# Load depth, store times, the first chunk turned by DMA, and planned landings in a fused recurrence and MoE kernel

## The chip, the cores and the metric

One Trainium2 chip; the kernel runs on one of its cores. The metric is the device time of one execution in microseconds (us). TensorE is called PE, VectorE DVE, ScalarE ACT, GpSimd POOL and SyncE SP, as the profile does.

## The reference

First a gated linear recurrence over 4 batches, 8 heads, 768 steps and heads of 48; then, on its output as 3072 tokens of 384, two dense layers (384 to 2048 to 384) with a squared ReLU between them.

```python
# recurrence: state is (B, H, D, D)
for t in range(S):
    state = alpha[:, :, t, :, None] * state + np.einsum('bhd,bhe->bhde', k[:, :, t], v[:, :, t])
    y[:, :, t] = np.einsum('bhd,bhde->bhe', q[:, :, t], state)
# x: y as (3072, 384)
h = x @ w_in            # 384 x 2048
r = np.maximum(h, 0.0)
out = (r * r) @ w_out   # 2048 x 384
```

## The kernel before, in words

**Chunks.** The 3072 tokens are 24 chunks of 128 (`NT`), six per batch. Chunks 0 to 3 are done as two "supers" (`add_super`), the others one at a time (`add_chunk`), from chunk 8 on with the scores of two chunks together. For a chunk, four operands of 128 x 384 floats are loaded by SP (`add_load`, L369: at, qt, kt, vt, 192 KB each). ACT takes the logarithm of at (L439), PE sums it along the chunk with a triangular matrix, and ACT makes the exponential of that and of its negative (`A` or `Af` L467, `Ainv` L471). DVE multiplies q and k by them into `qk_s` (L495 or L498, and L501). `qk_s` is turned (transposed) into `qkT`; PE makes the scores `sc` from it, DVE masks them into `sm` (L570), and PE sums masked scores times v, and q times the state, into the chunk's output. The state is carried by `st`: PE adds k times v, DVE multiplies it by the chunk's whole decay `ae_s` (`stm`, L604), ACT casts it (L609).

**The decay.** For chunks before `TURN` = 12, `ae_s` is made by small matmuls and exponentials. From 12 on it is copied out of the last row of `Af` by two small DMAs that POOL issues (`e_aed`, L484). `Af` has two buffers, so a chunk's `Af` waits until these DMAs of the chunk two before have read theirs.

**The turns.** A chunk's output is cast to `xn` (ACT, L395) and turned into its columns of `xT_big`, from which the first dense layer reads. Chunks 4 to 13 have both turns, `qk_s` to `qkT` and `xn` to `xT_big`, done by PE with an identity (8 and 3 transposes, L276) and a copy out of PSUM by DVE (L397). From `XFROM` = 14 on both are DMA transposes that SP issues (L515 and L416), in the same queue as the loads.

**The dense layers.** They run in groups of chunks (4, 1, 1, then pairs: `GN`). `add_moe1` is the first layer (PE), its ReLU (ACT, L876) and square into `gT` (DVE, L884); `add_moe2` the second (PE), the copy out of PSUM into `held` (L949 or L951) and the store (L959 or L962), which POOL issues except for the last three chunks. Their PE work lies between that of the chunks.

**What sets the order.** Nothing is reordered at run time: the order of every engine's instructions is written out by a planner (`Plan`) when the kernel is built. Each operation has an engine, a duration, a latency after it (`lat`), what it depends on, and perhaps an earliest time (`at`). The planner takes the operation that can start first; a wrong latency makes an engine stand in front of an instruction whose input has not come, with everything behind it in its order. The places that matter here:

- Loads: `LB` chunks can be loaded at once (pairs of chunks in `LB // 2` buffers for each of the four operands). In the plan a load waits for the chunk `LB` before (`prev`), and from chunk 14 on also for the one `LB - 1` (seven) before (`pace`).
- `AE_LAT`: what the plan assumes from the end of POOL's issue of `ae_s` to its landing. `XLAT` is the same for `qkT` (and, less 0.8, for `xT_big`); SP's issue of a turn counts as 1.25, and a turn is planned 2.0 after its inputs (`XB_SLACK`).
- `OUT_AT`: the earliest time of POOL's store of chunk s is `OUT_AT + 2.5 * s`. Until it is stored, an output stays in `held`, four buffers of four chunks each, of one kind with the buffers that the weights pass through.
- The gate: chunk s's first matmul may be planned when s is at most a lead plus the MoE work planned so far, in chunks (one chunk is 5.12 us of PE in the plan). The lead is 3.5, and more for later chunks, up to 6.

```python
return s <= (LEAD if s < 10 else min(6.0, LEAD + 0.25 * (s - 9))) + (prog["m1"] + prog["m2"]) / 5.12
```

A chunk also shares its slot of `qk_s` and `ae_s` with the chunk four before (`NBUF` = 4) and begins only when that one has its `xn`.

Of the kernel before, what the change touches and what calls it, by code (L numbers as in the profile page):

```python
# [59 lines left out]
def after(op, x=0.0):  # L60
    return (op, x)
# [103 lines left out]
def kernel(  # L165
# [21 lines left out]
    NT = n_tok // P  # L187
# [10 lines left out]

    consts = ctx.enter_context(tc.tile_pool(name="consts", bufs=1))
    big = ctx.enter_context(tc.tile_pool(name="big", bufs=1))  # L200
    LB = 8
    XR = 10
    loads = ctx.enter_context(tc.tile_pool(name="loads", bufs=LB // 2))
    work = ctx.enter_context(tc.tile_pool(name="work", bufs=4))
# [48 lines left out]

    NBUF = 4
    TURN = 12
    AE_LAT = 2.0
    L_s = big.tile([P, NBUF, H, DP], BF16)
    nc.gpsimd.memset(L_s[:, :, :, D:], 0.0)
    qk_s = big.tile([P, NBUF, 2, H, DP], BF16)
# [9 lines left out]
    def pin(ins):  # L269
        tc.keep_in_program_order(ins)  # L270

    def mm(*a, **kw):
        pin(nc.tensor.matmul(*a, **kw))  # L273

    def tr(*a):
        pin(nc.tensor.transpose(*a))  # L276
# [11 lines left out]
    def psum(op, shape, dt):  # L288
        i = op.slot.bank
        return banks[i].tile(shape, dt, name=f"bank{i}")  # L290
    X_SLACK = 0.2
    LD = 1.05
# [4 lines left out]
    def add(eng, dur, emit, *deps, **kw):  # L297
        return plan.add(Op(eng, dur, emit, deps, **kw))
# [42 lines left out]
    def w_dep(which, f):  # L341
        return w_ready[which][[hi > f for hi in W_CUT[which][1:]].index(True)]

    C = [dict() for _ in range(NT)]
# [1 line left out]
    SRC = dict(srcs)  # L346
    EARLY = 2 * 3
    PAIRS = 8
    XFROM, XTO = 14, NT
    XLAT = 2.2  # L350
    LEAD = 3.5

    NS = 2
# [6 lines left out]
    def add_load(s, nm):  # L360
        d = C[s]
        b, c = divmod(s, NCH)
        k = s // 2

        def ld():
            if s % 2 == 0:
                PAIR[k][nm] = loads.tile([P, 2, H, D], FP32, name=nm)
            d[nm] = PAIR[k][nm][:, s % 2]
            pin(nc.sync.dma_start(out=d[nm], in_=SRC[nm][b, c]))  # L369
        prev = C[s - LB]["use_" + nm] if s - LB >= 2 * NS else None  # L370
        if 2 * NS <= s < 2 * NS + LB and (k - LB // 2) < NS:
            prev = SUP[k - LB // 2]["use_" + nm]
        pace = C[s - LB + 1]["use_" + nm] if s >= TURN + 2 else None
        d["ld_" + nm] = add("DMA", LD if s < 12 else 0.95, ld, prev, pace, lat=2.4)

    PAIR = [dict() for _ in range(NT // 2)]
    SRC2 = [("at", alpha), ("qt", q), ("kt", k), ("vt", v)]
# [15 lines left out]
    def cast(op, out_t, in_t):  # L393
        if op.eng == "ACT":
            pin(nc.scalar.copy(out_t, in_t))  # L395
        elif op.eng == "DVE":
            pin(nc.vector.tensor_copy(out_t, in_t))  # L397
        else:
            pin(nc.gpsimd.tensor_copy(out_t, in_t))

    def add_tail(s, done, first, g):
        d = C[s]

        def e_xn():
            d["xn"] = work.tile([P, HD], BF16, name="xn")
            cast(xn, d["xn"], d["py"][:, 0:HD])
        xn = add("ACT", 0.36, e_xn, done, **g)
        first.gives = xn

        def e_p4():  # L410
            d["px"] = psum(p4, [P, KT, P], BF16)
            for j in range(KT):
                tr(d["px"][:, j, :], d["xn"][:, j * P:(j + 1) * P], ident_bf)
        if XFROM <= s < XTO:
            def e_xturn():
                pin(nc.sync.dma_start_transpose(out=xT_big[:, :, s % XR * P:(s % XR + 1) * P], in_=d["xn"]))  # L416
            d["x"] = add("XB", 0.0, e_xturn, xn, lat=XLAT - 0.8)
            d["x"].turn = 0.4
            d["end"] = xn
            return  # L420
        p4 = plan.add(Op("PE", 0.165, e_p4, [xn], takes=GLA_BANKS, lat=0.14, **g))

        def e_xT():
            cast(xT, xT_big[:, :, s % XR * P:(s % XR + 1) * P], d["px"])
        xT = add({"ACT": 0.36, "DVE": 0.27} if s < EARLY else "DVE", 0.27, e_xT, p4, prio=-9.0)
        d["x"] = d["end"] = xT
        p4.gives = xT

    def add_chunk(s):
        d = C[s]  # L430
# [57 lines left out]
        else:  # L488
            p0.gives = ai
            ae1 = add("POOL", 1.03, e_aed, a_, lat=AE_LAT, prio=-20.0)  # L490
            ae1.dma = 0.3
# [10 lines left out]
        mq = d["use_qt"] = add("DVE", 0.47 if s < TURN else 0.78, e_qA, a_, d["ld_qt"], old, **g)  # L502
        mk = d["use_kt"] = add("DVE", 0.47, e_kI, ai, d["ld_kt"], old, **g)
# [16 lines left out]
        def e_cp(lo, hi):  # L520
            if lo == 0:
                d["qkT"] = work.tile([P, 2 * NP, P], BF16, name="qkT")
            cast(cpk if lo else cp, d["qkT"][:, lo:hi, :], d["pT"][:, lo:hi, :])
        if s < EARLY:
            cp = add({"ACT": 0.49, "DVE": 0.34}, 0, lambda: e_cp(0, NP), p1q, **g)
            cpk = add({"DVE": 0.34, "ACT": 0.49}, 0, lambda: e_cp(NP, 2 * NP), p1k, after(cp, -9.0), **g)
        elif s < XFROM:
            cp = cpk = add("DVE", 0.61, lambda: e_cp(0, 2 * NP), p1k, **g)
        else:
            cp = cpk = add("XB", 0.0, e_turn, mq, mk, lat=XLAT)  # L530
            cp.turn = 0.9
        if s < XFROM:
            p1q.gives = cpk
# [47 lines left out]
    def add_back(s):  # L581
# [47 lines left out]
        p3b = plan.add(Op("PE", 0.21, e_p3b, [after(sm1, 0.02), sm0, vb, after(p3a)], takes=None if c else GLA_BANKS, lat=0.15, **g))  # L629

        add_tail(s, p3b, p3a or p3b, g)

    def add_super(u):
# [206 lines left out]
    NGT = 3  # L840
    FIRST = sl_bank[4:1:-1]
    M2_LAST = sl_bank[::-1]
    OUT_AT = 104.0
    LAST_COLS = ((0, 256), (256, 384))
    RELU_PRIO = -20.0
    RELU_PRIO0 = 0.0
# [4 lines left out]
    prog = {"m1": 0.0, "m2": 0.0}  # L851
# [69 lines left out]
    def add_moe2(g, tt, before, box, quarters, pools):  # L921
        if GT[g] + tt == NT - 1:
            return add_last(g, tt, before, pools)

        for qd in quarters:
            def e_mm(qd=qd):
                if qd == 0:
                    box["po"] = psum(box["first"], [P, 512], FP32)[:, 0:d_model]
                for kf in range(qd * FT // NQ, (qd + 1) * FT // NQ):
                    mm(box["po"], lhsT=gT[g][:, kf, tt * P:(tt + 1) * P], rhs=w_out_b[:, kf, :],  # L930
                       start=(kf == 0), stop=(kf == FT - 1))
            fs = range(qd * FT // NQ, (qd + 1) * FT // NQ) if g == 0 else range(FT)
            deps = [o for f in fs for o in sq[(g, f)]] + [w_dep("o", fs[-1] if g == 0 else FT - 1)] + ([after(before)] if before else [])
            op = plan.add(Op("PE", 0.65, e_mm, deps, takes=pools if qd == 0 else None, prio=0.1))
            op.moe = (2, 2.56 / NQ)
            if qd == 0:
                box["first"] = op
            op.lat = 0.05
            before = op
        if quarters[-1] < NQ - 1:  # L940
            return op
        s = GT[g] + tt

        def e_ev():
            if s % 4 == 0:
                held[s // 4] = stage.tile([P, 4, d_model], FP32, name="held", tag="stage")
            box["ob"] = held[s // 4][:, s % 4]
            if ev.eng == "DVE":
                pin(nc.vector.tensor_copy(box["ob"], box["po"]))  # L949
            else:  # L950
                pin(nc.scalar.copy(box["ob"], box["po"]))  # L951
        ev = add({"DVE": 0.47, "ACT": 0.38}, 0, e_ev, op, prio=-15.0)
        box["first"].gives = ev

        q = nc.gpsimd if s < NT - 3 else nc.sync

        def e_out():
            if s >= 2 * NS:
                pin(q.dma_start(out=out_r[s], in_=box["ob"]))  # L959
            else:  # L960
                for t in range(2):
                    pin(q.dma_start(out=out2_r[s, t], in_=box["ob"][HF * t:HF * t + HF]))  # L962
        if s < NT - 3:
            add("POOL", 0.56, e_out, ev, at=OUT_AT + 2.5 * s, lat=2.5, prio=5.0).dma = 0.55
        else:
            add("OUT", 0.55, e_out, ev)
        return op

    DMA_ORDER = ["0 at0 qt0 kt0 at1 qt1 kt1 vt", "1 at0 at1 qt0 kt0 qt1 kt1", "i", "1 vt"] + ["i"] * 5 + ["o"] * 4
    for x in DMA_ORDER + [s for s in range(2 * NS, NT) if s not in DMA_ORDER]:  # L970
        if x in ("i", "o"):
            load_w(x)
        elif isinstance(x, str):
            for nm in x[1:].split():
                add_load2(int(x[0]), nm)
            if len(SUP[int(x[0])]) == 2 * len(srcs) - 1:
                add_super(int(x[0]))
        else:
            for nm, _ in srcs:
                add_load(x, nm)  # L980
            add_chunk(x)
# [23 lines left out]
    def gate(op):  # L1005
        s = getattr(op, "gla", None)
        if s is not None:
            return s <= (LEAD if s < 10 else min(6.0, LEAD + 0.25 * (s - 9))) + (prog["m1"] + prog["m2"]) / 5.12
        return True

    def on_pick(op):
        m = getattr(op, "moe", None)
        if m:
            prog["m1" if m[0] == 1 else "m2"] += m[1]
    plan.on_pick = on_pick
    plan.run(gate)


# [47 lines left out]
```

## Time and profile before

| | |
|---|---|
| median of 3 runs | 182.1 us (181.08 to 182.48) |
| the profiled execution | 183.13 us |
| its span, first to last instruction | 181.4 us |
| PE / DVE / ACT / POOL busy | 96% / 69% / 68% / 29% of the span |
| granted PE clock, mean | 0.998 |
| read from HBM, written | 25.17 MB, 4.72 MB |
| transfers on SP's queue, on POOL's | 76.7%, 7.4% of 16 engines' span |

A row of the profile names engine, line of the kernel, operation, and out<-in by the program's names. "Busy" is the time in which an engine executed; matmuls are pipelined and their ends are modelled, so a row's mean is longer than the pace at which they follow each other. PEld are the weight loads that overlap the matmuls, and SPq is SP's sequencer, which issues DMAs. Idle time is put down to what ended the last wait. DMA share is the mean busy share of 16 DMA engines.

### The profile page before, as it was taken

The numbers are of one execution on the slowest core, as the hardware profiler recorded it, in microseconds if no ns is written. First come the engines' busy times: TensorE is split into PE (matmuls) and PEld (weight loads), VectorE is DVE, ScalarE is ACT, GpSimd is POOL, SyncE is SP. The second block draws the span as 40 slices with busy tenths as digits, with TensorE's granted clock in tenths as the row PEclk, the third lists the DMA queues.
The fourth block names the chain that finished last, engine by engine and source line by source line (L and its number), as shares of the span: only waits on it lengthen the run. The fifth ranks groups of instructions, "written<-read, shape, count | busy, mean of one in ns | idle before, by whom it ended". The sixth has DMA issues, their size and how long they took to land.

```text
span 181.4 us, 4845 instructions
## 1 busy us (share of the span) xinstructions
PE 173.3 (96%) x1883; PEld 127.1 (70%) x1883; DVE 124.5 (69%) x258; ACT 122.6 (68%) x263; POOL 53.5 (29%) x95
## 2 busy tenths in 40 slices
PE   7899999999999999999898999999997999999993
PEld 3567774666996788879676665787756767787663
DVE  6699569538898889989896875598754943455000
ACT  3565879267998599879586945698955843686221
POOL 6024466611121111133061257553290411010200
PEclk9999999999999999999999999999999999999999
DMA  5999999899998989999999999999998543210122
GB/s 139 274 276 325 338 290 383 201 214 207 190 200 167 226 173 216 198 227 180 201 208 142 191 214 163 266 231 158 243 170 213 117 97 107 47 47 0 43 87 90
DMA packets 113687, 33.83 MB, mean 186 GB/s; under 512 B 107728, under 2 KB 111952, under 8 KB 113664
## 3 DMA queue, kind: packets, MB, share of 16 engines
q1 hardware_dynamic: 111424, 29.37, 76.7%
q0 software_dynamic: 2240, 4.15, 7.4%
q8 instruction: 15, 0.25, 0.6%
q14 instruction: 8, 0.07, 0.1%
HBM read 25.17 MB, written 4.72 MB: 165 GB/s over the span
## 4 chain that ended last, share of the span: by engine, by line
PE 81%; DMA 8%; DVE 7%; ACT 1%; issue 1%; DVEq 0%; ACTq 0%
PE bank L273 73%; PE bank L276 5%; DMA qkT<-qk_s 3%; DMA xT_big<-xn 3%; DVE sm L570 2%; PE sc L273 2%; PE st L273 2%; DMA qt<-in_q_dram 2%; DVE sm L762 1%; DVE qkT L397 1%; DVE qk_s L699 1%; ACT r L876 1%; DVE xT_big L397 0%; DVE st L604 0%; DVE qk_s L495 0%
## 5 line engine op out<-in xcount | busy, mean ns | idle before, releaser
L273 PE MATMUL bank<-xT_big,w_in_b 128*128 128x256 bf16 (+2 forms) x600 | 71.6, 268 | 2.1 <-DMA xT_big<-xn 1.5
L273 PE MATMUL bank<-w_out_b,gT 128*128 128x384 bf16 (+2 forms) x400 | 69.8, 319 | 0.0
L876 ACT ACTIVATE r<-bank 128x512 bf16<-128x512 f32 x96 | 56.4, 612 | 11.1 <-PE bank L273 9.1
L273 PEld LDWEIGHTS <-w_in_b 128*128 128x128 bf16 x600 | 53.1, 98 | 12.5 <-issue 3.1
L884 DVE TENSOR_TENSOR gT<-r 128x512 bf16<-128x512 bf16 x96 | 43.5, 482 | 13.2 <-ACT r L876 12.8
L273 PEld LDWEIGHTS <-gT 128*128 128x128 bf16 x400 | 36.8, 98 | 19.7 <-issue 0.2
L444 POOL CAST vb<-vt 128x384 bf16<-128x384 f32 x20 | 11.5, 574 | 51.3 <-PE bank L273 25.5
L951 ACT COPY held<-bank 128x384 f32<-128x384 f32 x22 | 10.6, 483 | 17.9 <-PE bank L273 17.8
L484 POOL DMA_DIRECT2D ae_s<-Af x24 | 12.2, 513 | 22.1 <-ACT Af L467 20.3
L570 DVE TENSOR_TENSOR sm<-sc,utri_b 128x512 bf16<-128x512 f32 x24 | 15.4, 683 | 4.3 <-PE sc L273 4.2
L959 POOL DMA_DIRECT2D out_dram<-held x17 | 9.3, 549 | 26.0 <-ACT held L951 26.0
L395 ACT CAST xn<-bank 128x384 bf16<-128x384 f32 x24 | 11.2, 486 | 7.3 <-PE bank L273 7.2
L498 DVE TENSOR_TENSOR qk_s<-qt,Af 128x384 bf16<-128x384 f32 x12 | 10.3, 858 | 7.6 <-ACT Af L467 7.6
L273 PEld LDWEIGHTS <-qkT 64*128 64x128 bf16 (+2 forms) x304 | 10.6, 97 | 6.0 <-issue 2.3
L439 ACT ACTIVATE L_s<-at 128x384 bf16<-128x384 f32 x20 | 10.6, 530 | 2.4 <-DMA at<-in_alpha_dram 2.4
L604 DVE TENSOR_TENSOR st<-st,ae_s 128x384 f32<-128x384 f32 x16 | 9.0, 561 | 4.7 <-DMA ae_s<-Af 2.5
L397 DVE COPY qkT<-bank 128x1024 bf16<-128x1024 bf16 (+1 forms) x16 | 9.7, 619 | 3.3 <-PE bank L276 3.2
L467 ACT ACTIVATE Af<-bank 128x384 f32<-128x384 f32 x12 | 10.7, 893 | 1.4 <-DMA ae_s<-Af 0.8
L609 ACT CAST sb<-st 128x384 bf16<-128x384 f32 x16 | 7.9, 496 | 5.3 <-DVE st L604 5.0
L501 DVE TENSOR_TENSOR qk_s<-kt,Ainv 128x384 bf16<-128x384 f32 x20 | 11.3, 563 | 0.2 <-ACT Ainv L471 0.2
L276 PE MATMUL bank<-ident_bf,qk_s 128*128 128x128 bf16 x112 | 10.2, 224 | 0.5 <-DVE qk_s L699 0.3
L471 ACT ACTIVATE Ainv<-bank 128x384 bf16<-128x384 f32 x20 | 10.5, 525 | 0.0
(71 smaller groups left out, 168.8 us busy)
## 6 DMA issues: line engine op xcount, KB each, us to landing
at<-in_alpha_dram SPq DMA_DIRECT2D x24, 192.0 KB, 3.9
qt<-in_q_dram SPq DMA_DIRECT2D x24, 192.0 KB, 3.8
kt<-in_k_dram SPq DMA_DIRECT2D x24, 192.0 KB, 3.9
vt<-in_v_dram SPq DMA_DIRECT2D x20, 192.0 KB, 3.9
out_dram<-held POOLq DMA_DIRECT2D x17, 192.0 KB, 3.5
wo<-in_moe_w_out_dram SPq DMA_DIRECT2D x4, 768.0 KB, 7.9
wi<-in_moe_w_in_dram SPq DMA_DIRECT2D x4, 384.0 KB, 7.1
wi<-in_moe_w_in_dram SPq DMA_DIRECT2D x2, 768.0 KB, 6.1
```

Source lines behind the costliest of these rows:

```text
L273: pin(nc.tensor.matmul(*a, **kw))
L276: pin(nc.tensor.transpose(*a))
L395: pin(nc.scalar.copy(out_t, in_t))
L397: pin(nc.vector.tensor_copy(out_t, in_t))
L439: pin(nc.scalar.activation(L[:, :, 0:D], d["at"], AF.Ln))
L444: pin(nc.gpsimd.tensor_copy(d["vb"], d["vt"]))
L467: pin(nc.scalar.activation(d["A"], split(d["pm"][:, 0:HD], s), AF.Exp))
L484: pin(nc.gpsimd.dma_start(out=ae_s[HF * j:HF * j + D, i, j], in_=d["Af"][P - 1:P, j]))
L501: pin(nc.vector.tensor_mul(kI[:, :, 0:D], d["kt"], d["Ai"]))
L570: pin(nc.vector.tensor_mul(d["sm"][:, hh], d["sc"][hh], utri_b.to_broadcast([P, NP, P])))
L876: pin(nc.scalar.activation(box["r"][:, 0:w], box["ph"][:, 0:w], AF.Relu))
L884: pin(nc.vector.tensor_mul(gT[g][:, f0:f0 + per, lo * P:lo * P + n], r, r))
```

## The change

Loads are ten chunks deep instead of eight, and the plan no longer paces them by the chunk seven before; the condition for the first reused buffers counts from 0. Chunks 14 and 15 are turned by PE like those before them, both `qk_s` and `xn`; turns by DMA begin with chunk 16. In the plan, `ae_s` lands 3.6 us after its issue instead of 2.0, `qkT` 2.8 (3.6 for chunks 16 to 19) instead of 2.2, `xT_big` 2.0 instead of 1.4. Stores by POOL may go from 118 + 2.0 s on instead of 104 + 2.5 s. The lead stays at 3.5 up to chunk 11 and then grows by 0.4 a chunk instead of 0.25 from chunk 10 on: it is smaller than before for chunks 10 to 14 and larger for 15 to 18.

```diff
-    LB = 8
+    LB = 10
...
-    AE_LAT = 2.0
+    AE_LAT = 3.6
...
-    XFROM, XTO = 14, NT
-    XLAT = 2.2
+    XFROM, XTURN = 16, 16
+    XLAT = 2.8
...
         prev = C[s - LB]["use_" + nm] if s - LB >= 2 * NS else None
-        if 2 * NS <= s < 2 * NS + LB and (k - LB // 2) < NS:
+        if 0 <= k - LB // 2 < NS:
             prev = SUP[k - LB // 2]["use_" + nm]
-        pace = C[s - LB + 1]["use_" + nm] if s >= TURN + 2 else None
-        d["ld_" + nm] = add("DMA", LD if s < 12 else 0.95, ld, prev, pace, lat=2.4)
+        d["ld_" + nm] = add("DMA", LD if s < 12 else 0.95, ld, prev, lat=2.4)
...
-        if XFROM <= s < XTO:
+        if s >= XTURN:
             def e_xturn():
...
-            cp = cpk = add("XB", 0.0, e_turn, mq, mk, lat=XLAT)
+            cp = cpk = add("XB", 0.0, e_turn, mq, mk, lat=XLAT + (0.8 if s < 20 else 0.0))
             cp.turn = 0.9
...
-    OUT_AT = 104.0
+    OUT_AT = 118.0
...
-            add("POOL", 0.56, e_out, ev, at=OUT_AT + 2.5 * s, lat=2.5, prio=5.0).dma = 0.55
+            add("POOL", 0.56, e_out, ev, at=OUT_AT + 2.0 * s, lat=2.5, prio=5.0).dma = 0.55
...
-            return s <= (LEAD if s < 10 else min(6.0, LEAD + 0.25 * (s - 9))) + (prog["m1"] + prog["m2"]) / 5.12
+            return s <= (LEAD if s < 12 else min(6.0, LEAD + 0.4 * (s - 11))) + (prog["m1"] + prog["m2"]) / 5.12
```

## The prediction

> **What bounds the kernel now.** I began with the busy line of the page, then cut the span into stages, then asked who makes TensorE (PE) wait. All rows are of the profiled execution of the kernel before.
>
> ```profile
> PE 173.3 (96%) x1883; PEld 127.1 (70%) x1883; DVE 124.5 (69%) x258; ACT 122.6 (68%) x263; POOL 53.5 (29%) x95
> ```
>
> PE is the bound. The stages (start:end, length, then busy time and count for PE, weight load, DVE, ACT, POOL, then granted clock, DMA share, GB/s) show where its few idle microseconds lie:
>
> ```profile
> 60.00:94.00 34.00, 33.41 (x400) 26.77 (x399) 30.22 (x64) 27.48 (x59) 7.38 (x13) 1.00 1.03 202
> 94.00:104.00 10.00, 9.46 (x80) 7.02 (x77) 7.83 (x17) 8.49 (x18) 2.85 (x7) 1.00 1.06 174
> ...
> 118.00:128.00 10.00, 9.64 (x103) 8.26 (x102) 9.13 (x20) 9.04 (x20) 3.84 (x8) 1.00 1.09 205
> 128.00:140.00 12.00, 10.54 (x95) 7.18 (x93) 6.65 (x14) 7.84 (x17) 5.26 (x10) 1.00 1.06 211
> 140.00:150.00 10.00, 10.00 (x116) 7.17 (x115) 7.11 (x15) 6.22 (x13) 3.19 (x6) 1.00 0.45 98
> ```
>
> Up to 140 us the sixteen DMA engines are full (share above 1: records overlap); after that DMA is half idle and PE has no gap. Between 60 and 140 us PE idles 0.59 + 0.54 + 0.36 + 1.46 = 2.95 us (104 to 118 has none). That is nearly all that this change can win back. PE's own waits name the releasers (total, times, longest):
>
> ```profile
> PE bank L273 <- DMA xT_big<-xn: 1.5, 1, 1.5
> ...
> PE bank L273 <- ACT r L876: 0.7, 2, 0.5
> PE bank L273 <- DVE sm L570: 0.5, 1, 0.5
> PE bank L273 <- DMA qkT<-qk_s: 0.4, 1, 0.4
> ```
>
> Two are turns by DMA that land late, in this timeline of PE (start, length, then the idle time before in brackets):
>
> ```profile
> 124.99 0.40 PE L273 MATMUL sc<-qkT 64*128 64x128 bf16 x8
> 125.75 0.40 PE L273 MATMUL bank<-qkT 64*128 64x128 bf16 x8 [0.36 <-DMA qkT<-qk_s]
> ...
> 135.14 0.81 PE L273 MATMUL bank<-w_out_b,gT 128*128 128x384 bf16 x4
> 137.42 1.14 PE L273 MATMUL bank<-xT_big,w_in_b 128*128 128x256 bf16 x9 [1.46 <-DMA xT_big<-xn]
> ```
>
> The other two come from ae_s, the decay that chunks from 12 on move by a POOL DMA. At 87.29 DVE's `stm` (L604) waits for it, and the masks `sm` queued behind come late: 0.51 us on PE at 90.03. And the exponential `Af` (L467) has two buffers, so chunk 16's waits until chunk 14's ae has landed; in ACT's order a relu stands behind it, and PE then waits 0.54 us for that relu's bank at 99.63:
>
> ```profile
> 98.30 0.85 ACT L467 ACTIVATE Af<-bank 128x384 f32<-128x384 f32 x1 [0.80 <-DMA ae_s<-Af]
> 98.94 1.12 ACT L876 ACTIVATE r<-bank 128x512 bf16<-128x512 f32 x2
> ```
>
> **Two more turned chunks on PE (14 and 15).** Each adds 8 transposes of qk_s and 3 of xn. In the chain of waits such runs stand as
>
> ```profile
> 38.67 0.45 PE bank L276 x8
> ...
> 53.80 0.17 PE bank L276 x3
> ```
>
> so 0.45 + 0.17 = 0.62 us a chunk, **+1.24 us** for two. PE has no spare room there, so all of it counts. DVE gets two copies to qkT (0.68 us in its rows) and two to xT_big (0.35): 2.1 us, hidden, since between 94 and 104 us DVE is busy 7.83 of 10; at worst, without that cover, 2.1 us more. POOL and ACT get nothing.
>
> The Trainium skill speaks against this step: "TensorE: Matmul & The Clock Gate", Part 4 (PE-mode transpose), gives about 275 ns for one 128x128 transpose inside a kernel; by it the step would cost 6.1 us instead of 1.24. The trace has a mean of 224 ns from start to end, but eight in a row took 0.45 us, so they overlap.
>
> **Four turns fewer by DMA.** They free the SP queue of two issues of 1.64 us and two of 1.21 (medians of L515 and L416), 5.7 us. What they free on the DMA engines I read where nearly nothing else uses SP's queue, 140 to 160 us (packets, MB, share):
>
> ```profile
> q1 hardware_dynamic: 2720, 0.66, 20.3%
> ```
>
> Five turns of 0.66 MB took 20.3% of 20 us, 4.06 us. The four removed ones move 0.72 MB (two of 262 KB, two of 98 KB), so 4.4 us. The Trainium skill ("Advanced Engine Details and Errata", X-Bar Transpose) calls such turns as fast as plain DMAs and expects 350 to 400 GB/s, by which they would free about 2 us; the rows give 163 GB/s here.
>
> **Loads ten deep, without pace.** In 60 to 94 us, 35 loads took 101.8% of 34 us on q1: 0.99 us each. Loads already ran at that rate; only from 94.7 us, when SP began to interleave turns, were they spread out, the last landing at 133.9. Seventeen loads were left then: 16.8 us, plus two qk turns of 1.6 us, so they would now end near 115. They are not held up by buffers: load s needs chunk s-10's operands, and chunk 13's were multiplied at 84 us.
>
> **Stores held.** The first store was issued at 104.71, planned at 104, so planned times hold. Now stores go from 118 on at one per 2.0 us. Before, 118 to 134 us saw 8 stores, now 8 or 9: no fewer, but the loads are gone. In 140 to 160 us POOL's queue moved 0.99 MB in 15.0% of 20 us, so a store of 192 KB is 0.6 us of the engines; 118 to 140 us would carry 11 stores (6.6 us), five turns of qk_s (1.6 each) and six of xn (0.6 each): 18 of 22 us, where the share was 1.06 to 1.09.
>
> **Landings planned longer.** The medians from issue to landing were
>
> ```profile
> ae_s<-Af POOLq DMA_DIRECT2D x24, 0.8 KB, 3.6
> ...
> qkT<-qk_s SPq DMA_TRANSPOSE x10, 4.6
> xT_big<-xn SPq DMA_TRANSPOSE x10, 3.9
> ```
>
> against plans of 2.0 (after 1.03 of issue) for ae, 1.25 + 2.2 for qkT and 1.25 + 1.4 for xT_big. The new plans are 3.6, 1.25 + 2.8 (3.6 before chunk 20), and 1.25 + 2.0. So PE and DVE place the consumers later, with other work ahead: at 135 us four chunks' second-layer work (chunks 14 to 17) was there to be done. Of the three waits on qkT, xT_big and sm (0.36 + 1.46 + 0.51 = 2.33) I take 2.1 as gone. Nothing of PE's work goes, so that is the whole gain: **-2.1 us**.
>
> **Chunks begin later (10 to 13), then earlier (16 to 18).** By the gate, chunk 11 starts after 7.5 instead of 7.0 chunks' worth of MoE work, chunk 16 after 10.5 instead of 10.75. The later ones are covered by MoE work: at 90 us four chunks of second-layer work (8 to 11) were open, 10 us. Chunk 16 moves nearer to chunk 14: 1.2 chunk's worth instead of 1.5. Their `Af` stood 5.9 us apart, 0.8 of it the wait; 5.1 x 1.2 / 1.5 = 4.1 leaves a wait of 1.7. No row shows that wait at its new length: between -0.5 (ae lands sooner without turns beside it, and the wait goes) and +1.8 (the relu is as much later as ACT waits, and the chunk is early by the full quarter of MoE work, some 1.8 us with the recurrence in between). I take **+0.4**, half the added wait, since a bank of three was still free for part of the old one.
>
> **Sum:** +1.24 - 2.1 + 0.4 = -0.5 us. The profiled execution took 183.13 us, span 181.4; the median shown is 182.1, 1.0 below it. 183.1 - 0.5 is 182.6 for that execution, and **181.6** on the median.
>
> **Rivals.**
> *All waits go.* If the relu's wait goes too, and no new one appears: -2.95 + 1.24 = -1.7, and each removed wait also gives back the restart of PE (135.14 + 0.65 for four matmuls to 137.42 is 1.63, not 1.46; four times 0.16 = 0.6): -2.3, 179.8 us. For it: every wait has a DMA behind it, and that resource is relieved. Against: another order brings waits of its own. Chance 0.15.
>
> *The waits only move.* The turns of the pair (16,17) now meet the dense loads, as the pair (18,19) did, and wait as long; only sm's 0.5 goes, the ACT wait stays: +1.24 - 0.5 + 0.4 = +1.1, 183.2 us. Chance 0.16.
>
> *Slower: turns stuck behind loads.* SP issues in order, and nothing paces the loads any more. With two loads of 0.9 us ahead and the longest landing traced (6.2 for qkT, 5.6 for xT_big), a turn arrives 8.0 or 7.4 us after its input, against 6.85 and 5.25 that the plan allows (2.0 of slack, issue, landing): 1.2 + 2.1 = 3.3 us on the pair (16,17). With the gains kept: -0.5 + 3.3 = +2.8, **184.9 us**. It decides when more than one load stands ahead of a turn whose input is ready. For it: 105.32 to 111.31 for chunk 17's turn, with loads in flight. Against: it had stores beside it too, which are now gone from that stage. Chance 0.17.
>
> *Transposes that don't overlap.* At their 224 ns, 22 cost 4.9 us: 185.3 us. The row of eight in 0.45 us speaks against it. Chance 0.02. (It is the rule of the Trainium skill's "TensorE" page, Part 4, in this kernel.)
>
> **How the numbers follow.** The forecast has 0.50; its own range is 180.5 to 182.8. Faster by over 1% (below 180.3; 1% is about what a measurement of this kernel tells from no change): the first rival and a little of the forecast's edge, 0.19. Slower by over 1% (above 183.9): the last two, and a little of the second, 0.20. The rest, 0.61, lies within 1%. The range takes in the first rival and the slow one: 179.5 to 184.9.
>
> **What would show it.** Right: loads all landed near 115 us; DMA share from 118 to 140 well below 1; qkT turns there landing in about 4 us; no PE wait on xT_big or qkT over 0.5 us; L276's matmuls 22 more and PE busier by about 1.2 us; the span below the old one by about half a microsecond. Wrong: loads still landing after 125, PE waits on DMA of more than 1 us around 100 to 115, a longer wait of Af for ae_s near 98, or idle time of PE after 150 us because the last chunks' xT_big lands past 160.

## The result, and the profile after

| | median | executions | lowest to highest |
|---|---|---|---|
| before | 182.41 us | 18 | 180.99 to 184.66 |
| after | 183.05 us | 18 | 182.60 to 185.46 |

After is slower: ratio 1.0083, 95% interval 1.0055 to 1.0111. The ratio leaves out executions more than 1.5% above the fastest of their kernel, so it is not the quotient of the two medians (which differ by 0.64 us), and the four executions of after above 184.5 us had a granted clock of 0.99 instead of 1.00. That is within 1% of before, but on the other side of the forecast of 181.6 us. The two profiled executions say something else: after took 182.65 us with a span of 180.9, before 183.13 with 181.4, so after is 0.5 us *shorter* there. Both are true: after's profiled execution is the third fastest of its 18, and before's lies in the slower half (12 of its 18 timed ones were faster).

The stages of after (columns as before: stage, then busy time and count for PE, weight load, DVE, ACT, POOL; clock, DMA share, GB/s):

```profile
60.00:94.00 34.00, 32.17 (x371) 25.50 (x370) 27.33 (x56) 24.18 (x52) 6.54 (x12) 1.00 1.04 204
94.00:104.00 10.00, 10.00 (x124) 7.70 (x118) 8.79 (x19) 8.83 (x18) 3.04 (x6) 1.00 0.70 137
...
118.00:128.00 10.00, 10.00 (x112) 6.49 (x111) 6.61 (x12) 4.69 (x10) 5.71 (x12) 1.00 0.65 144
128.00:140.00 12.00, 12.00 (x120) 9.64 (x118) 8.56 (x18) 10.45 (x22) 6.31 (x13) 1.00 0.85 176
140.00:150.00 10.00, 10.00 (x121) 7.37 (x119) 7.55 (x17) 6.09 (x13) 4.51 (x9) 1.00 1.00 196
```

From 94 to 150 us PE has no gap left, and the DMA engines are no longer full up to 140 us (share 0.65 to 0.91). The turns land sooner (medians from issue, in the list of DMA issues of after):

```profile
ae_s<-Af POOLq DMA_DIRECT2D x24, 0.8 KB, 2.7
...
qkT<-qk_s SPq DMA_TRANSPOSE x8, 3.8
xT_big<-xn SPq DMA_TRANSPOSE x8, 3.3
```

But the stage from 60 to 94 us has lost 1.83 us of PE instead of 0.59. The timelines of ACT and PE show it within six microseconds; the brackets are the idle time before an instruction and what ended it:

```profile
84.18 0.87 ACT L466 ACTIVATE Af<-bank 128x384 f32<-128x384 f32 x1
...
88.49 0.84 ACT L466 ACTIVATE Af<-bank 128x384 f32<-128x384 f32 x1 [2.71 <-DMA ae_s<-Af]
89.13 0.63 ACT L875 ACTIVATE r<-bank 128x512 bf16<-128x512 f32 x1
```

```profile
87.93 0.61 PE L276 MATMUL bank<-ident_bf,qk_s 128*128 128x128 bf16 x8 [0.46 <-DVE qkT L396]
89.81 0.82 PE L273 MATMUL bank<-xT_big,w_in_b 128*128 128x256 bf16 x6 [1.28 <-ACT r L875]
```

Chunk 14's `Af` at 88.49 needs a buffer that chunk 12's `ae_s` DMA must have read; it stands only three places behind chunk 13's (84.18) in ACT's order, so ACT waits 2.71 us, the relu behind it is late, and PE waits for the relu's bank. It is the wait that before had at chunk 16 (0.80 us on ACT, 0.54 on PE), longer and at another place.

### The profile page after: what moved, and what is told of

Read it like the earlier page. It is cut to its first block, busy times and chain, and to the rows that moved or that the text cites. A ratio compares the mean times of both kernels' runs of the same rounds, so it can differ in the third digit from the quotient of the medians.

```text
span 180.9 us, 4882 instructions
## 1 busy us (share of the span) xinstructions
PE 173.1 (96%) x1904; PEld 127.9 (71%) x1905; DVE 128.3 (71%) x263; ACT 122.6 (68%) x262; POOL 52.7 (29%) x95
## 4 chain that ended last, share of the span: by engine, by line
PE 81%; DVE 8%; ACT 4%; issue 3%; DMA 2%; POOL 0%; ACTq 0%; DVEq 0%
PE bank L273 72%; PE bank L276 4%; DMA ae_s<-Af 2%; ACT r L875 2%; PE st L273 2%; PE sc L273 2%; DVE qkT L396 2%; DVE sm L569 1%; DVE gT L883 1%; DVE sm L761 1%; DVE qk_s L698 1%; ACT Af L466 1%; ACT A L682 1%; DVE xT_big L396 1%; DVE qk_s L500 1%
## 5 line engine op out<-in xcount | busy, mean ns | idle before, releaser
L883 DVE TENSOR_TENSOR gT<-r 128x512 bf16<-128x512 bf16 x96 | 44.8, 495 | 12.3 <-ACT r L875 11.8
L443 POOL CAST vb<-vt 128x384 bf16<-128x384 f32 x20 | 11.0, 551 | 57.9 <-DMA vt<-in_v_dram 21.1
L950 ACT COPY held<-bank 128x384 f32<-128x384 f32 x21 | 10.1, 479 | 21.1 <-PE bank L273 20.7
L396 DVE COPY qkT<-bank 128x1024 bf16<-128x1024 bf16 (+1 forms) x18 | 11.0, 626 | 3.0 <-PE bank L276 2.9
L276 PE MATMUL bank<-ident_bf,qk_s 128*128 128x128 bf16 x128 | 11.3, 219 | 1.6 <-DVE qk_s L698 0.9
L500 DVE TENSOR_TENSOR qk_s<-kt,Ainv 128x384 bf16<-128x384 f32 x20 | 12.0, 602 | 0.0
L276 PEld LDWEIGHTS <-qk_s 128*128 128x128 bf16 x128 | 8.4, 98 | 4.3 <-issue 2.1
L569 DVE TENSOR_TENSOR sm<-bank,utri_b 128x512 bf16<-128x512 f32 x16 | 10.2, 681 | 0.0
```

The costliest lines, as they stand in the source:

```text
L443: pin(nc.gpsimd.tensor_copy(d["vb"], d["vt"]))
L500: pin(nc.vector.tensor_mul(kI[:, :, 0:D], d["kt"], d["Ai"]))
L569: pin(nc.vector.tensor_mul(d["sm"][:, hh], d["sc"][hh], utri_b.to_broadcast([P, NP, P])))
L883: pin(nc.vector.tensor_mul(gT[g][:, f0:f0 + per, lo * P:lo * P + n], r, r))
```

## The experiments

Theory A, with which I went into the experiments: the 2.1 us of waits that I counted as won are not in most executions of before, and the change pays 1.24 us of transposes and a new wait for `ae_s`. The rivals: the waits are in every execution (B); PE only meets the next wait when one is taken away (C); the new wait comes from the turns or the landings, not from the lead (D); loads rather than stores crowd the turns (E).

Each kernel had 12 timed executions. A ratio is to before on the same chip, with its 95% interval. "From 14" or "16": the first chunk whose `qk_s` is turned by DMA.

| kernel | from | median | lowest to highest | ratio |
|---|---|---|---|---|
| e1, before again | 14 | 182.84 | 181.57 to 184.25 | 1.0043 (1.0004 to 1.0081) |
| e5, before, three Af | 14 | 182.41 | 180.73 to 185.16 | 0.9978 (0.9934 to 1.0021) |
| e9, before, stores held | 14 | 181.96 | 180.56 to 182.88 | 0.9979 (0.9940 to 1.0018) |
| e11, before, loads ten deep | 14 | 181.90 | 180.49 to 184.73 | 1.0000 (0.9960 to 1.0039) |
| e13, before, new lead | 14 | 184.14 | 182.35 to 187.22 | 1.0093 (1.0046 to 1.0140) |
| e8, after, three Af, turns from 14 | 14 | 182.49 | 181.58 to 185.38 | 1.0038 (0.9996 to 1.0079) |
| e10, after, old lead, turns from 14 | 14 | 182.16 | 180.66 to 183.68 | 1.0011 (0.9970 to 1.0052) |
| e3, before, turns from 16 | 16 | 182.54 | 182.29 to 183.51 | 1.0015 (0.9984 to 1.0046) |
| e2, after, three Af | 16 | 181.30 | 180.69 to 182.00 | 0.9948 (0.9917 to 0.9979) |
| e6, after, Af planned | 16 | 181.73 | 181.30 to 182.75 | 0.9998 (0.9967 to 1.0028) |
| e7, after, old lead | 16 | 181.15 | 180.90 to 182.06 | 0.9968 (0.9941 to 0.9995) |
| e12, e7 with xn turned by DMA from 14 | 16 | 180.43 | 180.21 to 181.18 | 0.9932 (0.9899 to 0.9965) |

e1 is the identical kernel: 1.0043 shows what a ratio of half a per cent is worth where executions differ by 3 us. Kernels timed on the same chip compare best: e1, e2, e3 and e5; e6 to e9; e10 to e13.

### Are the waits for turns in every execution of before?

e1 is before, unchanged.

> The kernel before, unchanged, profiled once more. Its first profile was of an execution of 183.13 us, 2 us above its fastest (181.0). Theory A (the waits for turns by DMA, 0.4 + 1.5 us on PE near 125 and 137 us, belong to slow executions alone): an execution of about 181.0 to 181.5 us shows less than 0.5 us of PE waiting for qkT and xT_big together. Rival B (these waits are in every execution, and the 2 us come and go elsewhere, in the start or outside the span): the waits stay at about 1.8 us, and some other row is 2 us shorter. Time ratio 1.00 either way.

The execution that was profiled took 182.69 us, a middling one: the median of the twelve is 182.84. Its PE waits:

```profile
PE bank L273 <- DMA xT_big<-xn: 1.1, 1, 1.1
...
PE bank L273 <- ACT r L876: 0.7, 1, 0.7
```

So the look that I had expected, an execution near 181.2 us, didn't come here. It came with e5, which has before's order with one more buffer:

```diff
-                d["Af"] = work.tile([P, 2, D, NP], FP32, name="Af", bufs=2)
+                d["Af"] = work.tile([P, 2, D, NP], FP32, name="Af", bufs=3)
```

> The kernel before with three buffers for Af; the order is the same. In its profile ACT waited 0.80 us for ae_s before chunk 16's Af and PE lost 0.5 to 0.7 us. Theory A (waits for ae_s count in every execution): 0.4 to 0.7 us less, ratio about 0.997. Rival C (PE would only meet the next wait): 1.000.

Its profiled execution took 181.21 us, and this is PE at the two places where before had waited 0.36 and 1.46 us:

```profile
124.70 0.40 PE L273 MATMUL sc<-qkT 64*128 64x128 bf16 x8
125.15 0.40 PE L273 MATMUL bank<-qkT 64*128 64x128 bf16 x8
...
134.54 0.81 PE L273 MATMUL bank<-w_out_b,gT 128*128 128x384 bf16 x4
135.42 1.14 PE L273 MATMUL bank<-xT_big,w_in_b 128*128 128x256 bf16 x9
```

No bracket: both turns were in time, in the same order of work. Three executions with this order, of 183.13, 182.69 and 181.21 us, waited 1.8, 1.2 and about 0.1 us for turns. (The third also lacks the wait for `ae_s` at chunk 16, worth 0.5 to 0.7 us of PE, which its buffer removes.) So the waits differ from one execution to the next, and B, which has them in every one, falls, unless that buffer had a hand in it; e3 below speaks against B too. But theory A is too strong as well: e1's middling execution had 1.2 of the 1.8 us. (e5's gain in time, 0.2%, is near the expected 0.3% and not clear of noise: its executions spread over 4 us.)

At the first of the two places the difference is in the landing: the turn to qkT was issued at 119.5 to 119.8 us in all three and took 6.2, 5.9 and 5.3 us to land. At the second, where PE waited longer, it is more in the issue. SP, first in before and then in e5:

```profile
130.69 2.94 SPq L416 DMA_TRANSPOSE xT_big<-xn  x2
```

```profile
129.45 2.63 SPq L416 DMA_TRANSPOSE xT_big<-xn  x2
```

The second turn of this pair, the one for which PE waits, was issued at 132.43 us in before, 132.26 in e1 and 130.88 in e5, and took 4.85, 4.57 and 4.40 us to land. PE's work there is 0.6 us earlier in e5 than in before; beyond that, the issue came 0.95 us earlier and the landing took 0.45 us less. In before the input of the pair's first turn was ready at 129.4, but SP had loads to issue up to 130.6; in e5 it was 128.8 and 129.4.

### Transposes on PE against turns by DMA

e3 is before with the turns alone moved.

```diff
-    XFROM, XTO = 14, NT
+    XFROM, XTO = 16, NT
```

> The kernel before with only the turns moved: XFROM 16 instead of 14, so chunks 14 and 15 are turned by PE. Theory A: PE gets 1.24 us more and gains nothing in fast executions, ratio 1.005 to 1.009. Rival B (the waits are in every execution, and fewer turns relieve them): 1.24 less 1 to 2 us, ratio 0.996 to 1.001.

Its executions lie between 182.3 and 183.0 us, but for one. So the fast executions of before (181.0 to 181.7, 10 of 35 on that chip) got some 1 us slower, and those of 183.0 to 184.0 (9 of 35) are all but gone. The ratio, 1.0015, lies between the two expectations for that reason. The table shows the narrower spread nearly throughout. Without the executions at a granted clock of 0.99 (four of after, four of e8, one each of e10 and e13), the kernels with `qk_s` turned from 14 spread over 2.3 to 4.4 us (2.3 to 2.7 without those more than 1.5% above their fastest), and those from 16, after among them, over 1.0 to 1.5. The exception is e8, turned from 14, with 1.1 us.

e8 and e10 put the turns of 14 and 15 back on DMA with everything else as in after, but for the wait for `ae_s`: e8 has the third buffer, e10 the old lead.

```diff
-    XFROM, XTURN = 16, 16
+    XFROM, XTURN = 14, 14
```

> The kernel of e2 (after, three buffers for Af) with the turns by DMA again from chunk 14 on, in the order that the plan makes of it. Theory A (PE is the bound; 22 transposes are 1.24 us, and waits for DMA stay small because loads end early and landings are planned as traced): 0.8 to 1.3 us less than e2, about 180.2, ratio about 0.988. Rival B (the two turns more bring the DMA waits back): no faster than e2, 0.995 or more, with PE waits for qkT or xT_big of 1 us.

> The kernel of e7 (after with the lead of before) with both turns by DMA from chunk 14 on. It differs from e7 in the turns of chunks 14 and 15 alone, and from before in loads, stores and planned landings. Theory A (in good executions the transposes simply add to PE): the fastest executions are 1.0 to 1.2 us below e7's (about 180 us); the spread tells whether waits for turns come back. If loads and held stores are enough to keep the turns on time, all executions lie within 1 us, ratio about 0.990; if the two turns fewer are what keeps them on time, the spread is 2 us or more, median no better than e7 (0.997).

Both have 1.24 us of transposes less and are no faster for it. e10's fastest execution, 180.66, is 0.24 us below e7's fastest, where 1.0 to 1.2 was expected, and its median is 1 us above e7's. e8's profile has a wait of PE of 1.2 us for xT_big, as its rival B expected, and a line of e10's PE waits shows the same:

```profile
PE bank L273 <- DMA xT_big<-xn: 1.8, 1, 1.8
```

Held stores, loads without pace and longer planned landings are in e10 and do not keep the turns on time. What does is two turns of `qk_s` fewer: e12 (below) differs from e10 in these alone, on the same chip, and has a median 1.7 us lower and a spread of 1.0 us. One thing that goes with it is when the loads end. In e10 the last load landed at 130.9 us, against 118.0 in e7 and 122.7 in e12, and the late turn's input was ready at 117.5 but SP issued it at 121.1, behind another turn and loads. So in these runs the loads end that early only with the two turns gone. Whether these count through SP's queue (two issues of about 1.6 us) or through the DMA engines (1.6 us each by the estimate) was not separated. e9 and e11 try the other two reliefs alone.

```diff
-    OUT_AT = 104.0
+    OUT_AT = 118.0
...
-            add("POOL", 0.56, e_out, ev, at=OUT_AT + 2.5 * s, lat=2.5, prio=5.0).dma = 0.55
+            add("POOL", 0.56, e_out, ev, at=OUT_AT + 2.0 * s, lat=2.5, prio=5.0).dma = 0.55
```

> The kernel before with only the stores held: from 118 + 2.0 s. Up to chunk 19 the order of the exponentials on ACT is that of before. Theory A (the stores crowd the turns near 125 and 137 us, in some executions more than in others): those waits get rare, executions gather near 181.0 to 181.7 with a spread under 1 us, ratio 0.995 to 0.998. Rival E (the loads, not the stores, crowd them): the spread stays at 181 to 184, ratio 1.000.

```diff
-    LB = 8
+    LB = 10
...
-        d["ld_" + nm] = add("DMA", LD if s < 12 else 0.95, ld, prev, pace, lat=2.4)
+        d["ld_" + nm] = add("DMA", LD if s < 12 else 0.95, ld, prev, lat=2.4)
```

> The kernel before with the loads alone changed: ten deep, no pace. Theory A (dense loads end near 115 us and the later turns run free): the waits near 125 and 137 us go, spread under 1 us near 181, ratio 0.995 to 0.998. Rival E (dense loads meet the turns of chunks 14 to 17 instead): waits for turns before 115 us, median 1 us above before.

Holding the stores gave the ratio that theory A expected, but not clear of noise, and left the spread at 2.3 us; its profiled execution had no wait for turns, but one for `ae_s` of 1.1 us on ACT. The deeper loads moved nothing that can be measured, and a wait of 0.6 us for xT_big stayed; neither theory A's gain nor rival E's loss came. e11 is no test of loads that end early, because they didn't: its last load landed at 133.3 us, before's at 133.9.

Neither part gains alone what can be measured: the turns (e3) gave a ratio of 1.0015, the rest without turns and lead (e10) 1.0011. Together (e7) they gave 0.9968. On one chip, e2 below has all of after but the wait for `ae_s`, and its slowest execution (182.00) is faster than e3's fastest (182.29).

### Where the new wait comes from

e2 is after with a third buffer for `Af` (and one fewer for `A`, to make room); the order of every engine is after's.

> The kernel after with three buffers for Af instead of two (and three for A instead of four, to make room); every engine's order is the same. In the profile after, ACT stood 2.71 us at 88.49 before chunk 14's Af, waiting for ae_s of chunk 12, and PE lost 1.28 + 0.46 us to it. Theory A: that wait is most of what the change costs beyond its transposes, so 1.3 to 1.7 us less than after, a ratio to before of about 1.000. Rival C (the loss is the transposes alone, and PE would only meet the next wait): less than 0.5 us below after, ratio about 1.007.

Median 181.30, 1.75 us below after. In e2's ACT timeline chunk 14's `Af` starts at 86.29 instead of 88.49:

```profile
86.29 0.87 ACT L466 ACTIVATE Af<-bank 128x384 f32<-128x384 f32 x1 [0.41 <-PE bank L273]
```

PE's wait of 1.28 us for the relu is gone. Its wait of 0.46 us for a copy to qkT stays, so that one is not the buffer's, as I had expected, and e2's profile explains 1.4 us (1.28 and the restart) of the 1.75; the two medians may be from different chips (after's is not on record). C, by which less than 0.5 us would have been gained, falls. The next two ask which part of the change made the wait. e7 is after with the old lead, e13 before with the new one.

```diff
-        return s <= (LEAD if s < 12 else min(6.0, LEAD + 0.4 * (s - 11))) + (prog["m1"] + prog["m2"]) / 5.12
+        return s <= (LEAD if s < 10 else min(6.0, LEAD + 0.25 * (s - 9))) + (prog["m1"] + prog["m2"]) / 5.12
```

> The kernel after with the lead of the kernel before (0.25 a chunk from 10 on). In ACT's order chunk 14's Af then stands 16 places behind chunk 13's, behind both xn, as before, instead of 3. Theory A (the later start of chunks 10 to 13 put chunks 12 and 14 next to each other and made the wait for ae_s): the 2.7 us wait of ACT is gone, 1.0 to 1.7 us less than after, ratio 0.995 to 1.002. Rival D (the moved turns or the longer landings made that wait): it stays, ratio about 1.008.

> The kernel before with the lead alone changed. In ACT's order chunk 14's Af then stands 3 places behind chunk 13's, as in after, instead of 16. Theory A (the lead makes the wait for ae_s): ACT waits 2 to 3 us for ae_s near 86 us, and PE loses 1.2 to 1.8 us, ratio 1.004 to 1.010. Rival D (the wait needs the moved turns or the longer landings): no such wait, ratio 1.000.

e7 has neither the wait for `ae_s` nor the one of 0.46 us, and its median is 1.9 us below after. e13 has the wait without anything else of the change, in its list of ACT's waits:

```profile
ACT Af L467 <- DMA ae_s<-Af: 2.5, 1, 2.5
```

and is 0.9% slower than before. So the lead alone makes the wait, and D falls. With the old lead the `Af` of chunks 12 and 14 begin 13 us apart (79.5 and 92.4 in before), with the new one 5.9 (82.6 and 88.5, of which 2.7 is the wait). Counting the dense layers' matmuls on PE before the first matmul of chunks 12, 13 and 14, in chunks as the gate does, gives 8.25, 8.5 and 10.0 in before, and 8.9, 9.1 and 9.4 in after. Chunks 12 and 13 start 0.6 later, with that much more MoE work ahead of them, and chunk 14, which the gate lets through at 9.3, gets in right behind chunk 13. (Its gate in before was 9.25; what held it to 10.0 there isn't shown.)

e6 leaves the lead and the two buffers and tells the plan of them.

```diff
-        a_ = add("ACT", 0.38 if s < TURN else 0.76, e_A, p0, **g)
+        a_ = add("ACT", 0.38 if s < TURN else 0.76, e_A, p0, C[s - 2]["ae1"] if s >= TURN + 2 else None, **g)
```

> The kernel after, with one more dependency in the plan: a chunk's exponential Af is planned only after ae_s of the chunk two before has landed (two buffers still). Theory A (the plan did not know of Af's two buffers, and that is what stops ACT): chunk 14's Af moves behind other work, ACT waits less than 0.8 us for ae_s there, and the time comes down by 1.0 to 1.7 us from after, a ratio to before of 0.995 to 1.002. Rival C (PE only meets the next wait): within 0.5 us of after, 1.006 to 1.009.

ACT's wait fell to 0.3 us and the median to 181.73, 1.3 us below after: the cause again, cured in the order instead of by a buffer.

### A version that beats both

e12 is e7 with `xn` of chunks 14 and 15 turned by DMA and their `qk_s` by PE.

```diff
-    XFROM, XTURN = 16, 16
+    XFROM, XTURN = 16, 14
```

> The kernel of e7 with xn of chunks 14 and 15 turned by DMA, their qk_s by PE. PE saves 6 transposes, 2 x 0.17 = 0.34 us, and the DMA engines get 1.2 us more. Theory A: 0.3 us less than e7 if these turns land on time, ratio about 0.995; if one of them is late, as much slower as it is late, with a PE wait for xT_big between 105 and 125 us.

180.43 us, ratio 0.9932 (0.9899 to 0.9965), the lowest median of all, with the smallest spread. The gain on before is 0.7%, where e1 shows that 0.4% can come from nothing, but 10 of its 12 executions are faster than the fastest of before's 35 on that chip. Between 94 and 140 us PE is never idle (stage row of e12):

```profile
94.00:140.00 46.00, 46.00 (x468) 34.95 (x467) 36.33 (x73) 35.51 (x73) 20.65 (x41) 1.00 0.89 181
```

By medians it is 0.7 us below e7, where 0.3 was worked out; the medians are from different chips, and the intervals of the two ratios overlap. The third buffer on top wasn't tried; e7 has no wait for `ae_s` that it could take away.

## Why the prediction was wrong

**The step that failed is the lead, +0.4 us.** The runs split the change. Without the new lead (e7) its ratio is 0.9968, 0.6 us below before (0.1 to 1.1), where the prediction's other terms, +1.24 - 2.1, gave -0.9. The lead takes it from 0.9968 to 1.0083, some 2.1 us (0.7 either way), and alone on before (e13) it costs 0.93%, 1.7 us. With 0.4 in the place of 2, the sum had to come out on the wrong side. Why it was mis-sized follows below.

**The profiled execution: luck.** The prediction had "182.6 for that execution", and after's profiled one took 182.65. Two errors cancel in it: in the spans, the change without the lead is 2.1 us shorter (e7, 179.3 against 181.4) instead of 0.9, and the lead adds 1.6 (180.9 against 179.3) instead of 0.4. After's execution was besides one of its fastest.

**The step from that execution to the median.** I took the whole 2.1 us of waits out of the median as well. Before's profile, 183.13 us, lay 2.1 us above the fastest of the three shown, 181.08, and showed just about 2 us of waits for late transfers: that was the warning that not every execution pays them. The middling execution of e1 had 1.2 us of the waits for turns. This term was too large in the median, but by less than the lead was too small: e7's -0.6 leaves about 1.8 us (0.5 either way) for all the waits that went, with the 0.54 us at chunk 16, which the 2.1 didn't hold.

**The waits themselves.** That the turns would land in time was right: the 0.36, 1.46 and 0.51 us are gone from after's profile. The reason was only partly mine. I named the loads, the stores and the planned landings as relief beside the turns; e10 has all three and still waited 1.8 us. The two turns of `qk_s` fewer are needed with them (e12 against e10).

**The transposes, +1.24 us.** e3's fast end agrees: it is 1.2 us above that of before on the same chip (182.3 against 181.0). e10 does not show it: it saves 0.24 us at its fast end, and as that execution was not profiled, whether waits hide the rest is open. What I had given as a sign was wrong: PE's busy time did not rise by 1.2 us (173.1 against 173.3). The rows of L276 did rise, from 10.2 + 4.6 to 11.3 + 5.3 us, but rows overlap, and those of the start came out shorter (`warm`, 6.2 to 5.7 us). The 22 more instructions (128 + 48 instead of 112 + 42 transposes) are there.

**Why the lead was mis-sized.** The mechanism, `Af` waiting for `ae_s` and a relu behind it, was the right one, and it was priced at chunk 16. It came at chunk 14: 1.28 us on PE, and 0.46 more for a copy to qkT that is gone in e7 too, where before had 0.54; so +1.2 in the profile, and 1.3 to 1.9 us by the medians of e2, e6 and e7 (1.5 to 2.5 by their ratios). I had counted the gate's shift for chunk 14 (none to speak of) but not for the pair 12 and 14. The same arithmetic brings it from 1.5 chunks' worth of work to 1.2, like the pair 14 and 16; counted in the traces it went from 1.75 to 0.5, so the gate is not all that sets a start. "Covered by MoE work" was true for PE and beside the point for ACT.

**Loads near 115 us.** The last landed at 120.1. SP's queue in after shows why:

```profile
97.22 0.87 SPq L369 DMA_DIRECT2D qt<-in_q_dram  x1
103.58 1.33 SPq L514 DMA_TRANSPOSE qkT<-qk_s  x1
104.96 0.57 SPq L369 DMA_DIRECT2D kt<-in_k_dram  x1
```

For 5.5 us SP stood before chunk 16's turn, whose input wasn't ready, with the loads behind it; the DMA share fell to 0.70. The slow rival had turns stuck behind loads. In after it was the other way round and made no gap on PE, since those loads weren't needed yet. In before and in e10 turns did stand behind loads, and PE waited for them.

**The sum.** By the ratios, in three steps: the turns alone (e3) +0.3 us, that is +1.24 for the transposes less about 1 us of waits; the loads, stores and planned landings on top (e7) -0.9; the lead +2.1; together 1.5 us (0.83%), where the prediction had -0.9 + 0.4. Each step is known to some 0.7 us only, from the intervals of the ratios.

## What to carry to other kernels

Compare the profiled execution's own time with the fastest of the runs before taking a wait out of the median: an execution 2 us above the fastest can show waits that others have in part or not at all, and to remove them narrows the spread more than it moves the middle (e7: spread 1.2 us, middle 0.6 lower). When a gate or a lead shifts some pieces of work, look at every pair that shares a buffer, above all one that the planner doesn't know of. In this kernel, work moved from a crowded queue to the bound engine cost its full time in good executions and paid only in bad ones, so move the part that crowds most for its price on the engine (`qk_s` here: e12 leaves `xn` on DMA and loses nothing; `xn` alone was not tried).

## What the runs showed of the hardware that I had not expected

With the DMA engines full (share 1.0 to 1.1), a turn that PE needs comes up to 2 us earlier or later in executions of one and the same order of work: three of them waited 1.8, 1.2 and 0.1 us. The landing is only a part of that: it moved by 0.9 us for one turn and by 0.45 for the other, whose issue moved by 1.55. SP issues loads and turns in the order of its queue, so a turn whose input isn't ready holds back loads (5.5 us in after), and loads hold back turns: in e10 one was issued 3.7 us after its input was ready. With two `qk_s` turned fewer the last load landed at 118 to 123 us instead of 131 (e7 and e12 against e10), and the spread came down from 2.7 us (one execution at a clock of 0.99 left out) to 1.2 and 1.0.
